# A second feed-forward layer recast in units of 768 tokens, with seven products for both of its matrices

## The chip, the core and the metric

The kernel runs on one core of a Trainium2 chip. The metric is device time in microseconds (us), from start to end of one execution; the median of several runs is compared. TensorE multiplies matrices into PSUM; VectorE, ScalarE and GpSimd (in the rows PE, DVE, ACT and POOL; PEld is TensorE's weight load) do elementwise work; SyncE (SP) issues nearly all DMA. Each engine runs its own instructions in program order and waits on semaphores of the others.

## What is computed

Attention over 4 x 8 heads of 576 tokens and 64 features with a block-causal mask, then two feed-forward layers on 2304 tokens of 512 features, all in float32 (cut from the reference):

```python
attn_out = _attn_ref(**attn_kwargs)             # 4 x 8 x 576 x 64
x = attn_out.transpose(0, 2, 1, 3).reshape(2304, 512)
h = x @ w_in                                    # layer 1: 512 x 2048
g = np.maximum(h, 0.0) + alpha * np.minimum(h, 0.0)
x = g @ w_out                                   # 2048 x 512
h = x @ w2_in                                   # layer 2
g = h * (1.0 / (1.0 + np.exp(-1.702 * h)))
out = g @ w2_out
```

The weights arrive as 64-bit floats. One product in float32 quality is made of three fast ones: each operand is split into a high part and the rest, and high x high, high x rest and rest x high are summed in PSUM. So every operand costs a copy on ScalarE (`hi_part`) and a subtraction on VectorE or GpSimd (`lo_part`) before TensorE can use it.

## The kernel before

The kernel has three stretches that overlap. **Attention** with the first half of layer 1 (8 of its 16 hidden blocks of 128) fills about the first 400 us. **Layer 1's late part** is the other 8 hidden blocks for all tokens, in units of 512 tokens (the order of units is 0, 1, 4, 2, 3, and unit 4 has 256 tokens). **Layer 2** is the same loop again over 5 units and all 16 hidden blocks, with another activation.

A late job is one pair of hidden blocks for one unit. Its first matrix is taken as a 2 x 2 block product with seven block products in place of eight: `comb` makes seven sums of weight blocks early and writes them to DRAM (`wcs`), `load_wc` brings the seven back for each job (7 DMAs of 256 KB), `comb_x` makes the seven sums of the input once per unit, and `prod` (line 838) runs one block product, six matmuls of 256 columns. `first_half`, `snap`, `second_half` and `sums` add the seven into two hidden blocks; `gate` and `gate_split` apply the activation and split it; `g2` (line 904) multiplies with the second matrix in the ordinary way, 12 matmuls of 512 columns for each hidden block. Unit 4 has only four block products per job. In layer 2 the second matrix is loaded, turned to float32 (`narrow`) and split (`split_w`) once, and stays on chip.

What sets the order: every step is put in a list with a place (`at`), and `arrange` (line 1080) plays the list through with a table of costs per instruction and fixes one order per engine; `SHIFT` (line 60) is a table of numbers added to the places, which act as priorities. Pools of tiles (`wts_b`, `xin`, `ps_o`, `ps_n`) open for the late part when attention has ended.

## Time and profile before

| | |
|---|---|
| median of 3 runs | 1004.02 us (1003.83 to 1005.17) |
| span of the profiled execution | 998.3 us |
| outside the span, median less span | 5.7 us |
| PE busy | 979.7 us, 98% |
| DVE busy | 596.3 us, 60% |
| ACT busy | 536.5 us, 54% |
| POOL busy | 359.1 us, 36% |
| DMA | 198.29 MB, mean 199 GB/s |

The span is one profiled execution, from its first to its last instruction. A matmul's busy time holds its way through the array, so matmuls in a stream overlap; what a matmul costs in a stream is read from the distance between starts. A row of the chain with xN is a run of N such matmuls, and its length divided by N is that distance.

### The profile page before, as it was taken

Reading aid. Unit: us, or ns where it says so; the run is one execution under the profiler, and the core shown is the slowest. Engines: PE = TensorE matmul, PEld = TensorE weight load, DVE = VectorE, ACT = ScalarE, POOL = GpSimd, SP = SyncE. Lnnn points to the kernel's source line nnn. Section 1 sums busy time; section 2 is a strip of 40 time slices with the busy share of each in tenths; the row PEclk is TensorE's granted clock in tenths of the full one; section 3 lists DMA queues with packets and bytes.
Section 4 is the critical chain, followed back from the end, with each engine's and each line's share of the span. In section 5 each row is a group of like instructions: output and inputs, shape, how many; then the busy total and the mean of one; then the engine's idle time right before and its main releaser. Section 6 shows DMA issues by size and latency. Waiting matters only on the chain.

```text
span 998.3 us, 21739 instructions
## 1 busy us (share of the span) xinstructions
PE 979.7 (98%) x8260; PEld 860.9 (86%) x8260; DVE 596.3 (60%) x1189; ACT 536.5 (54%) x1284; POOL 359.1 (36%) x396
## 2 busy tenths in 40 slices
PE   8999999999999999999999999999999999999998
PEld 5777877787888999999899989889999899899997
DVE  4788876786677564668777787665424423433321
ACT  4778777775777454555554555554424423433233
POOL 4346234442625156754435445243212411212000
PEclk9999999999999999999999999999999999999999
DMA  9645999999986866754655787986645756564360
GB/s 194 157 127 141 207 222 199 207 205 215 195 199 131 169 209 212 269 188 168 234 190 172 256 299 266 343 279 215 229 159 183 265 164 198 194 207 142 101 205 32
DMA packets 234646, 198.29 MB, mean 199 GB/s; under 512 B 146224, under 2 KB 172848, under 8 KB 234544
## 3 DMA queue, kind: packets, MB, share of 16 engines
q1 hardware_dynamic: 233216, 196.60, 69.2%
q8 instruction: 65, 1.06, 0.5%
q10 hardware_dynamic: 1328, 0.33, 0.2%
q14 instruction: 37, 0.30, 0.1%
HBM read 136.32 MB, written 40.89 MB: 178 GB/s over the span
## 4 chain that ended last, share of the span: by engine, by line
PE 84%; DMA 7%; ACT 3%; DVE 3%; SPq 1%; issue 1%; POOL 0%; ACTq 0%; DVEq 0%; POOLq 0%
PE acc L920 28%; PE ga L845 16%; PE ep L845 11%; PE h L225 8%; PE pv L601 3%; PE sc L450 3%; PE x L270 3%; PE x L271 3%; PE x L272 3%; DMA pt<-hl 3%; PE pv L526 2%; PE tp L390 1%; PE s L450 1%; DMA rw<-in_moe_w_in_dram 1%; PE et L492 1%; DMA xa<-xo 1%
## 5 line engine op out<-in xcount | busy, mean ns | idle before, releaser
L920 PE MATMUL acc<-wh,gs 128*128 128x512 f32 x576 | 184.6, 391 | 0.9 <-DVE o L930 0.9
L845 PE MATMUL ga<-xc,ws 128*128 128x256 f32 x1368 | 184.3, 283 | 0.0
L845 PEld LDWEIGHTS ga<-xc,ws 128*128 128x128 f32 x1368 | 176.3, 192 | 4.6
L845 PE MATMUL ep<-xc,ws 128*128 128x256 f32 x936 | 130.7, 284 | 0.0
L920 PEld LDWEIGHTS acc<-wh,gs 128*128 128x128 f32 x576 | 108.4, 188 | 22.8 <-DVE o L930 1.1
L871 POOL TENSOR_TENSOR v<-u,v 128x256 f32<-128x256 f32 x48 | 44.1, 918 | 229.2 <-ACT v L870 229.2
L845 PEld LDWEIGHTS ep<-xc,ws 128*128 128x128 f32 x936 | 120.6, 192 | 0.3
L920 PE MATMUL acc<-wl,gs 128*128 128x512 f32 x288 | 112.6, 391 | 0.0
L869 ACT ACTIVATE u<-ga 128x512 f32<-128x512 f32 x48 | 28.5, 594 | 148.5 <-PE ga L845 148.4
L143 DVE TENSOR_TENSOR gs<-g,gs 128x512 fp32r<-128x512 f32 (+1 forms) x80 | 65.1, 814 | 68.8 <-ACT gs L140 68.1
L143 POOL TENSOR_TENSOR gs<-g,gs 128x288 fp32r<-128x288 f32 x64 | 56.6, 887 | 101.8 <-ACT gs L140 98.1
L920 PE MATMUL acc<-gs,wh 128*128 128x512 f32 (+1 forms) x320 | 91.9, 370 | 0.5 <-DVE o L930 0.5
L140 ACT ACTIVATE gs<-g 128x288 fp32r<-128x288 f32 (+2 forms) x144 | 75.3, 524 | 19.9 <-DVE g L240 15.3
L225 PE MATMUL h<-xh,wh 128*128 128x288 f32 x256 | 79.1, 309 | 1.5 <-DVE g L240 1.5
L893 DVE TENSOR_TENSOR u<-ep,v 128x256 f32<-128x256 f32 x48 | 20.2, 421 | 99.0 <-PE ep L845 96.2
L270 PE MATMUL x<-gs,wh 128*128 128x288 f32 x256 | 77.5, 305 | 1.1 <-DVE g L240 0.6
L225 PE MATMUL h<-xlb,wh 128*128 128x288 f32 x256 | 77.5, 303 | 0.0
L225 PE MATMUL h<-xh,wl 128*128 128x288 f32 x256 | 76.6, 299 | 0.0
L271 PE MATMUL x<-gs,wh 128*128 128x288 f32 x256 | 76.4, 300 | 0.0
L272 PE MATMUL x<-gs,wl 128*128 128x288 f32 x256 | 76.4, 301 | 0.0
L464 DVE TENSOR_REDUCE stat<-sc 128x1 f32<-128x384 f32 (+7 forms) x128 | 55.1, 457 | 23.8 <-PE sc L450 23.5
L474 ACT ACTIVATE e<-sc,stat 128x384 f32<-128x384 f32 (+7 forms) x128 | 64.1, 511 | 7.4 <-DVE stat L464 6.7
(118 smaller groups left out, 2061.0 us busy)
## 6 DMA issues: line engine op xcount, KB each, us to landing
ws<-wc SPq DMA_DIRECT2D x284, 256.0 KB, 3.9
wc<-wc SPq DMA_DIRECT2D x84, 256.0 KB, 3.3
rw<-in_moe_w_in_dram SPq DMA_DIRECT2D x32, 512.0 KB, 4.2
rw<-in_moe_w_out_dram SPq DMA_DIRECT2D x32, 512.0 KB, 4.4
xa<-xo SPq DMA_DIRECT2D x32, 144.0 KB, 3.4
out_dram<-o SPq DMA_DIRECT2D x18, 256.0 KB, 2.4
nat_k<-in_k_dram SPq DMA_DIRECT2D x32, 128.0 KB, 3.1
vt<-in_v_dram SPq DMA_DIRECT2D x32, 128.0 KB, 3.2
```

What stands on the lines that cost most here:

```text
L140: act.activation(out=dst, in_=src, func=ACTF.Copy, scale=scale_)
L143: eng.tensor_tensor(out=dst, in0=src, in1=hi.bitcast(F32), op=ALU.subtract)
L225: pe.matmul(ps, st_[:, sl], mv[:, c], start=z == 0, stop=z == 3 * KD - 1)
L270: pe.matmul(ps, oh[:, sl], gh, start=f == 0, stop=False)
L271: pe.matmul(ps, oh[:, sl], gl, start=False, stop=False)
L272: pe.matmul(ps, ol[:, sl], gh, start=False, stop=f == NA - 1)
L450: pe.matmul(to[x:x + 64], qs[64 * h:64 * h + 64, 64 * y:64 * y + 64], ks[64 * h:64 * h + 64, k0:k0 + n], start=True, stop=True)
L464: dve.tensor_reduce(out=stat[:, 0, a:a + 1], in_=v, op=ALU.min, axis=AX.X if y < 8 else AX.XY)
L474: act.activation(out=eo if y < 8 else eo.rearrange("p (a b) -> p a b", a=2), in_=v, func=ACTF.Exp, scale=-1.0, bias=stat[:, 0, a:a + 1], a ...
L845: pe.matmul(ps, st_, mv, start=first and z == 0, stop=last and z == 5, skip_group_check=True)
L871: pool.tensor_tensor(out=v, in0=u[:, TH:TB], in1=v, op=ALU.subtract)
L920: pe.matmul(ps, a, b_, start=first and z == 0, stop=last and z == 2)
```

## The change

Layer 2 is written anew. Its tokens go in three units of 768, so a block product of the first matrix (`prod`) has 384 columns. All jobs of a unit run first; their activations stay on chip for the whole unit (`gb`, sixteen tiles of 768 columns). Then the second matrix is done as seven block products too: `g_sum` makes sums of the activations, `g_comb` splits them into one of seven slots, `t_load` and `t_split` bring the second matrix's sums, `g_prod` runs nine matmuls of 256 columns per block product, and `g_post` joins the four output quarters from the accumulators `a`, `b` and `d` and stores them. The second matrix's sums are made by `comb_t` in layer 1's late part and written to DRAM (`w2c` split, `w2s` whole). All weights of layer 2 come back through eight slots of 512 KB (`w_slot`), two block products to a DMA. The late tiles are ranges of bytes in a few large tiles (`late_tile`, `wquad`), some of them those of the early weights. `narrow` takes one form for both layers, which leaves out one VectorE instruction for each of layer 1's 32 weight tiles. The late part of layer 1 keeps its products. `SHIFT` has new numbers throughout, and `arrange` new costs for DMA.

```diff
-    "comb 2": 232.8, "comb 3": 44.7, "first": 27.1, "gate": -98.0, "gate 0": -19.6, "gate 2": 13.1,
...
+    "comb 2": 560.8, "comb 3": 4.3, "comb 4": -41.4, "first": 14.4, "first l0": 104.2, "first l1": 3.4,
...
-    TH = TB // 2
+    HB = TB // 2
+    TT = 768
+    TH = TT // 2
+    LOP = ()
+    WHOLE = (1, 2, 3)
...
+    w1s = [dram.tile([128, 7168], F32, name=f"wc1_{j}") for j in range(NPAIR[1] // 2)]
+    w2c = [dram.tile([128, 7168], F32, name=f"wk{j}") for j in range(NPAIR[1] // 2)]
+    w2s = [dram.tile([128, 3584], F32, name=f"wt{j}") for j in range(NPAIR[1] // 2)]
...
-        if u[0] == 0:
-            act.activation(out=sq, in_=wf[:, :, 1], func=ACTF.Copy, scale=2.0 ** -112)
-        else:
-
-            act.activation(out=sq, in_=wf[:, :, 1], func=ACTF.Prelu, scale=2.0 ** -112, alpha=2.0 ** 32)
...
-        if u[0] == 0:
-            dve.scalar_tensor_tensor(out=a, in0=hi, scalar=-0x80000000, in1=a, op0=ALU.bitwise_and, op1=ALU.bitwise_or)
...
+    def late_tile(tag, dtype=F32R):
+        if (tag, dtype) not in late:
+            n = {"s": 3584, "wo": 8192, "xa": 6144, "sc": 4608, "gs": 4608, "xl0": 2304, "xlb": 1152, "xh0": 1152}.get(tag, 4096)
+            src = late["n"] if tag in ("s", "wo", "xa", "sc") else blk if tag[0] in "gx" else wts_a
+            late[tag, dtype] = src.tile([128, n], dtype, tag=tag, name=f"l_{tag}")
+        return late[tag, dtype]
...
+    def sums_of(l, io, c11, c12, c21, c22, r):
+        if (l, io) == (1, 1):
+            return {4: (r, c12, c11, ALU.subtract), 6: (None, c22, c12, ALU.subtract), 5: (c11, c22, r, ALU.subtract),
+                    3: (None, c21, c11, ALU.subtract)}, {0: c11, 1: c21, 2: c22}
+        return {4: (r, c21, c22, ALU.add), 6: (None, c11, c21, ALU.subtract), 5: (c11, r, c11, ALU.subtract),
+                2: (None, c12, c11, ALU.subtract)}, {0: c11, 1: c12, 3: c22}
...
+    def comb_t(j, z):
+        i = MAKE[z]
+        a, b = (words[1, f, 1] for f in fpair(1, j))
+        if i == 0:
+            words[1, j, "r"] = raw.tile([128, 256], F32, tag="wr", bufs=1, name="wr")
+        two_, one_ = sums_of(1, 1, *quarters(a, b), words[1, j, "r"])
+        whole = i in WHOLE
+        t = wc_tile((1, 2 * j, 1), whole)
+        if i in two_:
+            r, x, y, op = two_[i]
+            if r is None:
+                r = t[:, 1] if whole else t[:, 1].bitcast(F32)
+            (dve if i % 2 else pool).tensor_tensor(out=r, in0=x, in1=y, op=op)
+        else:
+            r = one_[i]
+        if whole:
+            o = 512 * i + 256 * (j % 2)
+            sp.dma_start(out=w2s[j // 2][:, o:o + 256], in_=r)
+        else:
+            hi_part(t[:, 0], r)
+            lo_part(pool if i % 2 else dve, t[:, 1], r, t[:, 0])
+            o = 1024 * i + 512 * (j % 2)
+            sp.dma_start(out=w2c[j // 2][:, o:o + 512], in_=t.bitcast(F32).rearrange("p h c -> p (h c)"))
...
+        z = 512 * (7 * (j % 2) + PORD.index(i))
+        sp.dma_start(out=w1s[j // 2][:, z:z + 512], in_=t.bitcast(F32).rearrange("p h c -> p (h c)"))
...
+    def w_slot():
+        z = w_at[0] % 8
+        w_at[0] += 1
+        t = wquad(z - 1)[:, 3072:4096] if z in (1, 2) else late_tile("xa")[:, 1024 * (z and z - 2):][:, 0:1024]
+        return t.rearrange("p (y h c) -> p y h c", y=2, h=2)
...
+    def load_x(u):
+        for z in range(4):
+            r, h = z // 2, z % 2
+            t = late_tile("w2", F32)[:, 768 * z:768 * z + 768].rearrange("p (c t) -> p c t", c=2)
+            xr[u, z] = t
+            sp.dma_start(out=t, in_=x2s[256 * r:256 * r + 256, u + TH * h:u + TH * h + TH].rearrange("(c p) t -> p c t", p=128))
...
+        two_ = {4: (r, b12, b11), 6: (b12, b22, b12), 5: (b11, b22, r), 3: (b21, b21, b11)}
+        one_ = {0: b11, 1: b21, 2: b22}
+        if i in two_:
+            x, y0, y1 = two_[i]
+            pool.tensor_tensor(out=x, in0=y0, in1=y1, op=ALU.subtract)
+        else:
+            x = one_[i]
+        z, o = {0: (late_tile("xl0"), 0), 4: (late_tile("s"), 0), 5: (late_tile("s"), 1536), 1: (wquad(0), 0), 6: (wquad(0), 1536),
+                2: (wquad(1), 0), 3: (wquad(1), 1536)}[i]
+        t = z[:, o:o + 1536].rearrange("p (h c t) -> p h c t", h=2, c=2)
+        hi_part(t[:, 0], x)
+        lo_part(dve, t[:, 1], x, t[:, 0])
+        xc[u, i] = t
...
+    def prod(ps, w, x, first, last):
+        z = 0
+        for c in range(2):
+            sl = slice(128 * c, 128 * c + 128)
+            for st_, mv in ((w[:, 0, sl], x[:, 0, c]), (w[:, 0, sl], x[:, 1, c]), (w[:, 1, sl], x[:, 0, c])):
+                pe.matmul(ps, st_, mv, start=first and z == 0, stop=last and z == 5, skip_group_check=True)
+                z += 1
...
+    def part_a(p):
+        u, j = jobs[p]
+        late_buffers()
+        a, d = (cbank()[:, 0:TH] for _ in range(2))
+        b = bank("b")[:, 0:TH]
+        job[p] = [a, b, d]
+        for i, ps, first in ((0, a, True), (5, b, True), (4, d, True), (1, a, False)):
+            prod(ps, jw.pop((p, i)), xc[u, i], first, i == 1)
+            if i == 0:
+                t = jt[3 * (p % 2)]
+                act.activation(out=t, in_=a, func=ACTF.Copy)
+                job[p].append(t)
+            if i == 5:
+                t = jt[3 * (p % 2) + 1]
+                dve.tensor_tensor(out=t, in0=b, in1=job[p][3], op=ALU.add)
+                job[p].append(t)
+
+    def part_b(p):
+        u, j = jobs[p]
+        a, b, d, p1, uu = job[p][:5]
+        prod(b, jw.pop((p, 6)), xc[u, 6], False, False)
+        q = jt[3 * (p % 2) + 2]
+        dve.tensor_tensor(out=q, in0=b, in1=p1, op=ALU.add)
+        c22 = gb[2 * j + 1][:, TH:]
+        dve.tensor_tensor(out=c22, in0=d, in1=q, op=ALU.add)
+        job[p].append(c22)
+
+    def part_c(p):
+        u, j = jobs[p]
+        a, b, d, p1, uu = job[p][:5]
+        prod(d, jw.pop((p, 2)), xc[u, 2], False, True)
+        c12 = gb[2 * j][:, TH:]
+        dve.tensor_tensor(out=c12, in0=d, in1=uu, op=ALU.add)
+        prod(b, jw.pop((p, 3)), xc[u, 3], False, True)
+        c21 = gb[2 * j + 1][:, 0:TH]
+        dve.tensor_tensor(out=c21, in0=b, in1=p1, op=ALU.add)
+        job[p] += [c12, c21]
...
+    def g_sum(u, j, i):
+        two_, _ = gsum(u, j, i)
+        o, x, y, op = two_[i]
+        dve.tensor_tensor(out=o, in0=x, in1=y, op=op)
+
+    def g_comb(u, j, i):
+        two_, one_ = gsum(u, j, i)
+        x = two_[i][0] if i in two_ else one_[i]
+        t = gc_slot()
+        hi_part(t[:, 0], x)
+        lo_part(dve, t[:, 1], x, t[:, 0])
+        gcs[u, j, i] = t
...
+    def t_split(u, j, i):
+        r, t = gw.pop((u, j, i)), w_slot()
+        hi_part(t[:, :, 0], r)
+        lo_part(pool if i in LOP else dve, t[:, :, 1], r, t[:, :, 0])
+        for y in range(2):
+            gw[u, j + y, i] = t[:, y]
...
+    def g_prod(u, j, i):
+        key = {0: "a", 1: "a", 5: "b", 6: "b", 3: "b", 4: "d", 2: "d"}[i]
+        first, last = i in (0, 5, 4) and j == 0, i in (1, 3, 2) and j == NPAIR[1] - 1
+        if first:
+            acc[u, key] = [cbank() for _ in range(2)]
+        ps = acc[u, key]
+        g, w = gcs.pop((u, j, i)), gw.pop((u, j, i))
+        for m in range(3):
+            sl = slice(128 * m, 128 * m + 128)
+            o = 256 * (m % 2)
+            to, ops = ps[m // 2][:, o:o + 256], ((g[:, 0, sl], w[:, 0]), (g[:, 0, sl], w[:, 1]), (g[:, 1, sl], w[:, 0]))
+            for z, (st_, mv) in enumerate(ops):
+                pe.matmul(to, st_, mv, start=first and z == 0 and m != 1, stop=last and z == 2, skip_group_check=True)
...
+                dve.tensor_tensor(out=t[:, x:y], in0=ps, in1=(acc[u, "p1"] if i in "uq" else t)[:, x:y], op=ALU.add)
+        if i in ("p1", "u", "q"):
+            return
+        r, h = int(i[0]), int(i[1])
+        sp.dma_start(out=out[u + TH * r:u + TH * r + TH, 256 * h:256 * h + 256].rearrange("(m p) d -> p m d", p=128),
+                     in_=t.rearrange("p (m d) -> p m d", m=3))
...
+    for u in range(0, NT, TT):
+        at("load x", n - (9 if u else 4.5), lambda u=u: load_x(u), L)
+        for z, i in enumerate(XORD):
+            at("split x 2", n - 3 + 0.4 * z, lambda u=u, i=i: comb_x(u, i), L)
+        for j in range(kp):
+            p = len(jobs)
+            jobs.append((u, j))
+            m = n + J * j
+            for z in range(14):
+                if z % 2 == 0 and z // 7 == j % 2:
+                    y = z % 7
+                    at("load wc", m - 1.5 + Q * y + (0.6 if y > 4 else 0), lambda p=p - j % 2, c=z // 2: job_w(p, c), L)
+            at("first", m, lambda p=p: part_a(p), L)
+            at("snap", m + 1.2, lambda p=p: part_b(p), L)
+            c = J + 0.8 if j < kp - 1 else 1.25
+            at("second", m + c, lambda p=p: part_c(p), L)
...
+        seq = [(j, 0) for j in range(kp)]
+        seq += [(j + y, i) for j in range(0, kp, 2) for i in (5, 4) for y in range(2)]
+        seq += [(j, i) for i in (6, 1, 2, 3) for j in range(kp)]
+        for z, (j, i) in enumerate(seq):
+            m = n + Q * z
+            lag = 1.5
...
+    seq_w += [(t_end + NR + 1 + (n2 + 14 - t_end - NR) * j / NPAIR[1], 1, 0, j) for j in range(NPAIR[1])]
+    seq_w += [(n2 + 15 + (n3 + 4 - n2 - 15) * j / NPAIR[1], 1, 1, j) for j in range(NPAIR[1])]
...
-                t = size / run * (8.3 + 0.0368 * run) / 16
+                t = size / run * (12 + 0.0415 * run) / 16
```

In layer 2 before, TensorE's row of work for one job (`ga` and `ep` are the job's two PSUM banks, `xc` and `ws` sums of input and weights, `acc` the output, `wh` and `wl` the second matrix's parts):

```order
L845 MATMUL ga<-xc,ws 128x256 x12
L845 MATMUL ep<-xc,ws 128x256 x6
L845 MATMUL ga<-xc,ws 128x256 x12
L845 MATMUL ep<-xc,ws 128x256 x12
L920 MATMUL acc<-wh_9775,gs 128x512
L920 MATMUL acc<-wl_9776,gs 128x512
L920 MATMUL acc<-wh_9775,gs 128x512 x2
```

In the changed kernel, TensorE where the last job of the second unit (L1094, accumulators `b` and `c`) meets that unit's products of the second matrix (L1210; `l_sc` holds the split activations, `l_xa` and `w` the slots of weights):

```order
L1094 MATMUL b<-w_651,w_745 128x384 x6
L1094 MATMUL c_10599<-w_651,w_745 128x384 x6
L1210 MATMUL c_10681<-l_xa,l_sc 128x256 x6
L1210 MATMUL c_10682<-l_xa,l_sc 128x256 x3
L1210 MATMUL c_10681<-l_xa,l_sc 128x256 x6
L1210 MATMUL c_10682<-l_xa,l_sc 128x256 x2
L1094 MATMUL b<-w_745,l_xa 128x384 x6
L1210 MATMUL c_10682<-l_xa,l_sc 128x256
```

The 512-column matmuls of layer 2 are gone; job after job of 384 columns is followed by a long run of 256-column products.

VectorE in such a run of products of the first unit, in the changed kernel (L160 is a split: of activations into `l_sc` or `l_xl`, of weights from `st`; L1166 is a sum of activations, L1225 joins an output):

```order
L160 TENSOR_TENSOR l_xa<-st,l_xa 128x2x256
L160 TENSOR_TENSOR l_sc<-l_w_8887,l_sc 128x384
L160 TENSOR_TENSOR l_xa<-st,l_xa 128x2x256
L160 TENSOR_TENSOR l_xl_8728<-l_w_8887,l_xl_8728 128x384
L1166 TENSOR_TENSOR l_w_8887<-l_w_8887 128x384
L160 TENSOR_TENSOR l_sc<-l_wo,l_sc 128x384
L1166 TENSOR_TENSOR l_w_8887<-l_w_8887 128x384
L1166 TENSOR_TENSOR l_wo<-l_wo,l_w_8887 128x384
L160 TENSOR_TENSOR l_sc<-l_wo,l_sc 128x384 x4
L1225 TENSOR_TENSOR l_gs<-c_9568,l_gs 128x512
```

And before, VectorE in a job of layer 2 (`wl` is the split of the second matrix, `gs` that of the activations, `wa` and `sq` the turning of weights to float32):

```order
L893 TENSOR_TENSOR u<-ep,v 128x256
L894 TENSOR_TENSOR u<-u,ga 128x256
L895 TENSOR_TENSOR ep<-ep,u 128x256
L896 TENSOR_TENSOR ga<-ga,u 128x256
L143 TENSOR_TENSOR wl_9449<-sq,wh_9448 128x512
L143 TENSOR_TENSOR gs<-g,gs 128x512
L175 TENSOR_SCALAR wa<-sq 128x512
```

The splits of activations, four sums and one split per weight tile have become seven splits and four sums per pair of hidden blocks and the splits of three of the seven weight sums in every unit.

## Rows read from the trace of the kernel before

**Rows 1.** Windows: busy us (instructions) of each engine, granted clock, DMA share, GB/s
```profile
core 0: us, PE busy (x) PEld busy (x) DVE busy (x) ACT busy (x) POOL busy (x), PEclk, DMA share, GB/s
400.00:600.00 200.00, 198.95 (x1330) 183.86 (x1329) 147.68 (x273) 105.88 (x231) 99.36 (x106) 1.00 0.66 223
0.00:350.00 350.00, 337.56 (x4108) 271.42 (x4108) 252.85 (x584) 243.54 (x682) 140.37 (x174) 0.99 0.84 183
...
600.00:650.00 50.00, 49.12 (x313) 44.59 (x312) 34.28 (x62) 29.88 (x54) 20.55 (x20) 1.00 0.85 303
650.00:994.00 344.00, 344.00 (x2149) 311.92 (x2147) 131.98 (x229) 129.32 (x256) 68.70 (x69) 1.00 0.56 184
```
**Rows 2.** The chain of work that ended last: start, length, what
```profile
392.31 6.41 PE h L225 x48
...
845.42 1.44 PE ep L845 x12
846.86 5.47 PE acc L920 x24
```
**Rows 3.** Groups by line: form and count, busy us, mean ns, idle before
```profile
L920 PE MATMUL acc<-wh,gs 128*128 128x512 f32 x576 | 184.6, 391 | 0.9 <-DVE o L930 0.9
L845 PE MATMUL ga<-xc,ws 128*128 128x256 f32 x1368 | 184.3, 283 | 0.0
...
L845 PE MATMUL ep<-xc,ws 128*128 128x256 f32 x936 | 130.7, 284 | 0.0
...
L920 PE MATMUL acc<-wl,gs 128*128 128x512 f32 x288 | 112.6, 391 | 0.0
```
**Rows 4.** Timeline, PE where layer 2 begins: start, length, what [idle before]
```profile
599.01 1.60 PE L845 MATMUL ga<-xc,ws 128*128 128x256 f32 x12
...
633.50 0.50 PE L920 MATMUL acc<-wh,gs 128*128 128x512 f32 x1 [0.88 <-DVE o L930]
```
**Rows 5.** Timeline, the end: ACT's copies and SP's stores
```profile
993.70 1.28 ACT L933 ACTIVATE o<-acc 128x512 f32<-128x512 f32 x2 [3.23 <-PE acc L920]
...
994.32 1.02 SPq L934 DMA_DIRECT2D out_dram<-o  x2
```
**Rows 6.** Timeline of DVE around 578 us
```profile
575.72 0.69 DVE L143 TENSOR_TENSOR xc<-xt,xc 128x512 fp32r<-128x512 f32 x1
576.32 0.68 DVE L143 TENSOR_TENSOR gs<-ga,gs 128x512 fp32r<-128x512 f32 x1
...
580.44 0.41 DVE L894 TENSOR_TENSOR u<-u,ga 128x256 f32<-128x256 f32 x1
580.77 0.42 DVE L895 TENSOR_TENSOR ep<-ep,u 128x256 f32<-128x256 f32 x1
```
**Rows 7.** Groups of DVE by line, 400 to 600 us
```profile
L179 DVE SCALAR_TENSOR_TENSOR sq<-rw,wa 128x512 int32<-128x512 int32 x17 | 13.5, 793 | 0.3
...
L143 DVE TENSOR_TENSOR wc<-wc 128x256 fp32r<-128x256 f32 x21 | 10.1, 482 | 9.5 <-ACT wc L140 9.3
...
L175 DVE TENSOR_SCALAR wa<-sq 128x512 int32<-128x512 int32 x17 | 8.6, 508 | 1.9 <-ACT sq L173 1.0 <-DMA wc<-wc 0.8
L747 DVE TENSOR_TENSOR wc<-sq 128x256 f32<-128x256 f32 x14 | 8.4, 599 | 3.6 <-DMA wc<-wc 3.5
```
**Rows 8.** Windows of 10 us, as rows 1
```profile
570.00:580.00 10.00, 10.00 (x64) 9.04 (x63) 9.89 (x17) 5.53 (x11) 6.81 (x6) 1.00 0.77 245
580.00:590.00 10.00, 10.00 (x74) 9.47 (x74) 8.94 (x19) 5.79 (x12) 2.95 (x4) 1.00 1.03 359
```
**Rows 9.** Timeline, DVE and POOL in one job of layer 2
```profile
880.17 0.74 POOL L872 TENSOR_TENSOR u<-u,v 128x256 f32<-128x256 f32 x1
...
880.22 1.23 DVE L143 TENSOR_TENSOR gs<-g,gs 128x512 fp32r<-128x512 f32 x1 [0.73 <-ACT gs L140]
...
889.29 0.69 DVE L143 TENSOR_TENSOR gs<-g,gs 128x512 fp32r<-128x512 f32 x1 [1.66 <-ACT gs L140]
```
**Rows 10.** What PE waited for, 0 to 350 us: total, times, longest
```profile
PE pv L601 <- DMA pt<-hl: 5.5, 7, 2.0
```

More of the change, by code (lines that the diff above doesn't have):

```diff
@@ L922, in block_out @@
[L922 to L934 removed]
+            for z, (a, b_) in enumerate(((oh[:, sl], gh), (oh[:, sl], gl), (ol[:, sl], gh))):
+                pe.matmul(accs[key][d][:, 0:n], a, b_, start=first and z == 0, stop=last and z == 2)
@@ new lines, in job_gate, with gsum @@
+    def job_gate(p, y):
+        u, j = jobs[p]
+        g = gb[2 * j + (y == 2)]
+        to = (g[:, 0:TH], g[:, TH:], g)[y]
+        act.activation(out=to, in_=job[p][0] if y == 0 else to, func=ACTF.Gelu_apprx_sigmoid)
+    gcs = {}
+    gw = {}
+    def gsum(u, j, i):
+        t0_, t1_ = gb[2 * j], gb[2 * j + 1]
+        h = slice(0, TH), slice(TH, 2 * TH)
+        c11, c12, c21, c22 = t0_[:, h[0]], t1_[:, h[0]], t0_[:, h[1]], t1_[:, h[1]]
+        r = g1[j % 2]
+        sub, add = ALU.subtract, ALU.add
+        two_ = {4: (r, c21, c22, add), 6: (c21, c11, c21, sub), 5: (c11, r, c11, sub), 2: (c12, c12, c11, sub)}
+        return two_, {0: c11, 1: c12, 3: c22}
@@ L959 @@
-        if j == NPAIR[l] - 1:
+            at("gemm2", place[p + 2] + 0.1 + 0.1 * y, lambda u=u, f=f, a=j == 0 and y == 0, b=j == NPAIR[0] - 1 and y == 1: g2(u, f, a, b))
+        if j == NPAIR[0] - 1:
             at("out", place[p + 2] + 0.4, lambda u=u: block_out(u))
     for u in units:
-        n = start[u[3]]
-        at("load x", n - 8, lambda u=u: load_x(u))
-        for y, i in enumerate(XC if u[2] == TB else (0, 1)):
-            at("split x 2", n - 2 + 0.1 * y, lambda u=u, i=i: comb_x(u, i))
@@ L968 @@
[L968 to L972 removed]
+        n = start[u[2]]
+        at("load x", n - 8, lambda u=u: load_x1(u))
+        for y, i in enumerate(XC if u[1] == TB else (0, 1)):
+            at("split x 2", n - 2 + 0.1 * y, lambda u=u, i=i: comb_x1(u, i), after=n - 0.08 + 0.01 * y if i in (1, 3, 4, 6) else None)
```

474 lines of the change are left out of this document (293 added, 181 removed), and 6 rows, old and new, of the table SHIFT.

## The prediction

> **What bounds the kernel now.** I read the windows first. In 650 to 994 us, which is layer 2 alone, PE is busy in all 344.00 us, while DVE is busy in 131.98, ACT in 129.32 and POOL in 68.70 of them, and the DMA share is 0.56 [rows 1]. So there the time is the number of matmuls times their distance, and nothing else. From 400 to 600 us PE is busy in 198.95 of 200, but DVE already in 147.68 (74%) [rows 1]. In the first 350 us PE is idle for 12.4 us (350 less 337.56), and the largest single wait behind that, 5.5 us in seven pieces, is for a DMA of the attention [rows 1, 10]. The granted clock is 0.99 to 1.00 in all of these, the upper of the two levels, so the clock has nothing to give [rows 1]. The kernel is bound by PE, and a change pays by taking distance out of PE's row. It pays for as long as the other engines can prepare operands at the new pace.
>
> The busy time of a group does not give that distance: one 512-column matmul counts as 391 ns busy [rows 3], yet 24 of them in the chain take 5.47 us, so 227.9 ns each [rows 2]. Twelve of 256 columns take 1.44 us, so 120 ns, and 48 of 288 columns take 6.41 us, so 133.5 ns [rows 2]. I work with these. There is no row for 384 columns. Its distance lies between the last one and 227.9; on the straight line between 288 and 512 columns (0.421 ns a column) it is 133.5 + 96 x 0.421 = 174.0 ns.
>
> **PE's work in layer 2.** Before: the 576 + 288 matmuls of 512 columns whose moving operand is the second layer's `gs` [rows 3] take 864 x 0.2279 = 196.9 us. Of L845 there are 1368 + 936 = 2304 in all [rows 3]; layer 1 has 16 full jobs of 42 and 4 small ones of 24, 768, which leaves 1536 x 0.120 = 184.3 us. Together 381.2 us. As a test of this arithmetic: layer 2's first matmul starts at 599.01 [rows 4] and the last output copies begin at 993.70, the last store at 994.32 [rows 5], so some 395.3 us. In them lie also the last two `g2` of layer 1, 48 x 0.228 = 10.9 us, and 3.2 us remain for idle time, of which 0.88 is one wait for a DVE copy [rows 4]. So the sum accounts for the stretch to 1%.
>
> After: 24 jobs of seven block products of six matmuls are 1008 x 0.174 = 175.4 us, and three units of 56 block products of nine are 1512 x 0.120 = 181.4 us, 356.8 us together. **PE gains 24.4 us.** Most comes from the second matrix: seven products in place of eight, and no unit of 256 tokens with its four products for three quarters of the gain of seven. If 384 columns cost 165 or 183 ns (5% either way), this is 9 us more or less.
>
> **What the other engines must do for it.** One unit of 768 tokens now takes PE 58.5 us of jobs (8 x 7.31) and 60.5 us of products, 119.0 us. DVE starts instructions of 512 columns 0.60 us apart (575.72 to 576.32) and of 256 columns 0.33 us apart (580.44 to 580.77) [rows 6], which puts 384 columns at 0.465 and 768 at 0.87 us. For one unit: 8 jobs x 5 additions x 0.465 = 18.6; 32 sums of activations x 0.465 = 14.9; 56 splits of them x 0.465 = 26.0; 12 splits of weight sums x 0.60 = 7.2; 5 joins of the output, 0.93 each, 4.7; 7 splits of the input x 0.87 = 6.1. That is 77.5 of 119.0 us, 65%, and so it fits on the whole. The halves differ: in a unit's products alone (nearly all sums, the splits, the weights, the joins, part of the input) I count some 55.9 of 60.5 us, 92%. So there is a slack of 4.6 us in each such half, and the order must be good. ACT has one copy for each split and less of the rest, about 40 of 67 us where they are densest; it follows DVE.
>
> How firm are DVE's durations? The same 512-column split took 1.23 us at 880.22, beside an addition on POOL at 880.17, and 0.69 us at 889.29 with none there [rows 9]. The Trainium skill (GPSIMD Engine Reference, section 1, Specifications) says that GpSimd shares its SBUF interfaces with VectorE and that the two contend when a VectorE instruction has two SBUF inputs, as these splits have; that pair of rows agrees with it. In the changed kernel POOL has almost nothing in the products but the next unit's input sums, so I keep the short durations and make the long one a rival.
>
> Between jobs and products PE meets operands that depend on the last job's activation, and at a unit's end the accumulators must be joined before their banks are used again. The program's row of work interleaves there: the last job's `b` waits while products of earlier hidden blocks run. Three units have two such places each. A wait like the 0.88 us of [rows 4] at half of them is 3 us; nothing at all is the one bound, 2 us at each of six places, 12 us, the other. **I take +3.**
>
> **Layer 1's late part.** The second matrix's preparation moves here. From 400 to 600 us 17 narrowings ran [rows 7]; eleven more come in from later, each 0.508 + 0.793 us, 14.3 us. The sums and splits of `comb_t` add for seven pairs about 2 x 0.599 + 3 x 0.48 us each, 18.5 us; eight of L747's go, 4.8 us [rows 7]. So DVE goes from 147.68 [rows 1] to about 176 of 200 us, 88%. That is close, but the work has a whole layer's length to be done in, and in 570 to 580 us PE was busy in 10.00 us beside a DVE busy in 9.89 [rows 8], so a dense DVE does not by itself hold PE up. Bounds: 0 where it all fits, and 12 us where the part above 88% turns into delay of the gates in half of the jobs. **I take +3.** The new DMA writes go on SP's queue; the share there was 0.66 [rows 1].
>
> **The weights' way back.** A job of layer 2 reads 1.835 MB. Before, a full job took 42 x 0.120 + 24 x 0.228 = 10.5 us with its `g2`; now jobs follow each other every 7.31 us, so 251 GB/s in the job halves and less in the products. The trace moved 303 GB/s over 600 to 650 us at a share of 0.85 [rows 1] and 359 over 580 to 590 [rows 8]. So I take 0 here, with the eight slots of 512 KB in front as the cover; without it, see the second rival.
>
> **The start and the end.** L178's 32 instructions go, 24.7 us of DVE in all (0.77 each), but no wait of PE in the first 350 us that I found ends with them; the longest sum of waits is for `pt` [rows 10]. DVE was busy there in 252.85 of 350 us [rows 1]. I put that at 0. The new numbers in `SHIFT` reorder the attention as well, though PE's work there is the same: the 12.4 us of idle time may shrink (at best by about 8, since the first loads are needed in any order) or grow as much. **I take -1.** At the end two copies by ACT (1.28 us for both) and a store of 256 KB stand last [rows 5]; after it are a join by DVE of 512 and 256 columns, 0.93 us, and a store of 384 KB. **+0.8**, between 0 and 2.
>
> **Sum.** 998.3 - 24.4 + 3 + 3 - 1 + 0.8 = 979.7 us of span. Around the span lie 5.7 us (median 1004.02 less 998.3). So **985.4 us**, 1.9% faster. The terms' own bounds are wide in the late part and the joins (0 to 12) and in the start (-8 to +8); all would hardly fall to one side, and I give this case 975 to 992.
>
> **The rivals.**
>
> First, VectorE sets the pace of the products. If the 56 splits start 0.62 us apart and not 0.465, a third longer, where POOL's neighbourhood alone made one 1.8 times as long [rows 9], a half needs 55.9 + 8.7 = 64.6 us against PE's 60.5. That is 4.1 us three times, 12.3; it takes the place of the 3 us for joins: 994.7, still faster. It decides from 4.6 us more per half. For it speak the 92%; against it, that POOL is idle for most of these halves and that the sums can begin while jobs still run.
>
> Second, the slower side: the weights' feed sets the pace of the jobs. The gain of 18.6 us (1004.0 - 985.4) is eaten when each of 24 jobs takes 0.78 us longer, 8.08 us, which is 227 GB/s. At 220, hardly under what 400 to 600 us moved with 0.66 of the engines [rows 1], a job takes 8.34 us, 24.8 us are lost, and the time is 1010. For it: reads and stores and the next unit's input share the queues, and a slot can be refilled only when the product that reads it has ended, so eight slots are four products' worth of time in practice. Against it: the 303 and 359 GB/s [rows 1, 8].
>
> Third, the attention's new order gives back most of PE's idle time there: -8 in place of -1, so 978.
>
> Fourth, the change doesn't bring what it counts: the late part and the joins both near their bound of 12, 985.4 + 18 = 1003.4, no change.
>
> Fifth, the distance of matmuls may not go by columns as I took it. With fewer columns per matmul something is lost if long matmuls are the cheaper ones per column. In these rows 512 columns cost 0.445 ns each, 288 cost 0.464 and 256 cost 0.469 [rows 2], so the loss is small and is in the sum. Were a 512-column matmul much cheaper, the gain on PE would vanish and only the +5.8 us of the other terms would stay: 1009.8. The Trainium skill (TensorE: Matmul & The Clock Gate, section Back-to-back issue gap) gives, for sustained streams, about 81 ns for 128 columns and 131 ns for 512; on a line between these, 256 and 384 columns would be 98 and 114 ns, and layer 2 would go from 263.2 to 262.9 us, an estimate from that page: no gain. The rows show 120 and 227.9 ns and speak against it.
>
> **How the numbers follow.** Forecast, 975 to 992: 0.66. VectorE's pace, about 995: 0.14. Feed, about 1010: 0.08. Attention, about 978 and below: 0.07. No change, about 1003: 0.03. The distance rule, 1009.8: 0.02. About 0.2% is what a measurement of this kernel can tell from no change, 2 us here. Faster is forecast, VectorE's pace and attention, less a hundredth for a VectorE worse than priced: 0.86. Same, 0.04. Slower, feed and rule: 0.10. The range runs from 974 to 998: below, a little under the attention's case; above, just over VectorE's; it leaves out the last three cases and some of each tail.
>
> **What would show it.** In the changed profile the chain should hold runs of 384 columns at 174 ns a matmul; layer 2 from its first matmul to its last should take about 360 us with PE busy in all but a few of them; and 400 to 600 us should have a DVE near 88% and PE still above 97%. Idle time before L1210 put down to DVE's or ACT's splits would mean the first rival; idle time before L1094 put down to DMA the second; fewer than 6 us of idle time in the first 350 us the third. I am wrong if the 384 columns are off the line, or if the late part of layer 1 turns DVE's load into waits of PE beyond 12 us.

## The result, and the profile after

The changed kernel takes 980.1 us (median of four runs, 978.9 to 983.8), 0.977 of the kernel before (95% interval 0.974 to 0.980). Forecast were 985.4 us, within 974 to 998. A second set of runs gave 981.6 us and 0.979 (0.976 to 0.981). The profiled execution spans 977.0 us, 21.3 less than before.

The windows of the changed kernel, in the stretches of [rows 1] (columns as there):

```profile
core 0: us, PE busy (x) PEld busy (x) DVE busy (x) ACT busy (x) POOL busy (x), PEclk, DMA share, GB/s
0.00:350.00 350.00, 339.71 (x4128) 272.69 (x4129) 237.88 (x562) 245.66 (x688) 144.18 (x175) 1.00 0.81 185
...
400.00:600.00 200.00, 197.97 (x1322) 182.68 (x1323) 172.83 (x318) 119.99 (x261) 109.46 (x120) 1.00 0.82 280
600.00:650.00 50.00, 49.44 (x261) 45.60 (x260) 35.62 (x58) 21.50 (x38) 14.48 (x9) 1.00 0.93 340
650.00:970.00 320.00, 319.97 (x2299) 319.65 (x2298) 227.71 (x429) 161.11 (x305) 11.91 (x6) 1.00 0.69 226
```

PE is as full as before; what shrank is its row of work. VectorE (DVE) is the engine that grew: 228 of 320 us in layer 2, where it was 132 of 344, and 173 of 200 us in the late part of layer 1, where it was 148.

Layer 2 by halves of its three units (jobs, then products, from the first unit's jobs on):

```profile
608.00:677.70 69.70, 69.70 (x396) 67.27 (x396) 44.47 (x75) 29.04 (x52) 10.46 (x8) 1.00 0.87 303
677.70:734.30 56.60, 56.60 (x473) 56.60 (x473) 50.99 (x100) 32.79 (x65) 4.13 (x2) 1.00 0.64 216
734.30:796.80 62.50, 62.50 (x371) 62.50 (x370) 34.08 (x59) 26.52 (x47) 3.89 (x2) 1.00 0.82 277
796.80:853.40 56.60, 56.60 (x473) 56.60 (x472) 49.94 (x100) 32.70 (x65) 0.00 (x0) 1.00 0.65 207
853.40:913.50 60.10, 60.07 (x347) 59.75 (x347) 29.33 (x55) 20.95 (x38) 0.00 (x0) 1.00 0.79 257
913.50:972.60 59.10, 59.10 (x495) 59.10 (x494) 47.83 (x97) 33.35 (x66) 0.00 (x0) 1.00 0.45 141
```

In the products DVE is busy for some 50 of 56.6 us, nine tenths, while PE never stops. From the chain of waits, the rows that answer [rows 2] (start, length, what):

```profile
677.68 56.63 PE c L1210 x472
734.31 1.04 PE c L1094 x6
735.36 1.04 PE b L1094 x6
...
738.48 1.04 PE c L1094 x6
...
740.05 1.07 PE c L1094 x6
...
853.39 1.04 PE c L1094 x6
```

472 matmuls of 256 columns in 56.63 us are 120.0 ns each. Six of 384 columns take 1.04 us, 174 ns by the distance of their starts. From the second unit's first job (734.31) to the third's (853.39) are 119.08 us; 58.5 + 60.5 = 119.0 were counted. The only waits of PE behind the late part of layer 1, and the end (timeline of DVE and SP):

```profile
PE b L1094 <- ACT l_s L157: 0.6, 1, 0.6
```
```profile
972.57 1.02 DVE L1225 TENSOR_TENSOR l_gs<-c,l_gs 128x512 f32<-128x512 f32 x2 [6.21 <-PE c L1210]
973.62 0.37 SPq L1229 DMA_DIRECT2D out_dram<-l_gs  x1
```

**Where the 21.3 us came from.** I cut each trace in three, at the first matmul of layer 2 and at the last matmul. What PE still has to do for layer 1 at the first cut (matmuls left times their distance) is counted to the part ahead.

| us | before | after | difference | forecast |
|---|---|---|---|---|
| first matmul of layer 2 | 601.2 | 599.0 | | |
| work of layer 1 left there | 10.9 | 14.6 | | |
| ahead of layer 2 (sum of the two) | 612.1 | 613.6 | +1.5 | -1 + 3 |
| layer 2 (rest, to the start of the last matmul) | 381.9 | 359.0 | -22.9 | -24.4 + 3 |
| from there to the end of the span | 4.3 | 4.4 | +0.1 | +0.8 |
| span | 998.3 | 977.0 | -21.3 | -18.6 |

The line of layer 2 is firm and the line ahead of it is not. By the same cut layer 2 of the kernel before takes 381.5 and 382.4 us in two other runs below (the one in the old order and the one with a planner cost moved; 386.8 in a third, with a new plan), and layer 2 of the changed kernel takes 357.3 to 359.0 us in all seven runs that leave it as it is. The part ahead ends at 616.2 us when the changed kernel runs again, so there +1.5 could as well be +4.1.

### The profile page after: what moved, and what is told of

The parts are those of the page before. It is cut to its first block, busy times and chain, and to the rows that moved or that the text cites. A ratio compares the mean times of both kernels' runs of the same rounds, so it can differ in the third digit from the quotient of the medians.

```text
span 977.0 us, 22224 instructions
## 1 busy us (share of the span) xinstructions
PE 957.8 (98%) x8380; PEld 870.1 (89%) x8380; DVE 699.0 (72%) x1405; ACT 574.7 (59%) x1353; POOL 311.3 (32%) x341
## 5 line engine op out<-in xcount | busy, mean ns | idle before, releaser
L1210 PE MATMUL c<-l_xa,l_sc 128*128 128x256 f32 x1026 | 129.0, 283 | 0.0
L1210 PEld LDWEIGHTS c<-l_xa,l_sc 128*128 128x128 f32 x1026 | 126.2, 192 | 0.0
L256 PE MATMUL h<-xh,w 128*128 128x288 f32 x512 | 113.5, 305 | 2.8 <-DVE g L285 2.7
L1010 PE MATMUL c<-gs,l_wo 128*128 128x512 f32 (+1 forms) x480 | 108.8, 371 | 0.6 <-ACT gs L157 0.4
L256 PEld LDWEIGHTS h<-xh,w 128*128 128x128 f32 x512 | 83.7, 188 | 12.2 <-issue 6.9
L1010 PEld LDWEIGHTS c<-gs,l_wo 128*128 128x128 f32 x480 | 82.1, 189 | 13.6 <-ACT gs L157 0.8
L160 POOL TENSOR_TENSOR gs<-g,gs 128x288 fp32r<-128x288 f32 x64 | 57.5, 903 | 93.7 <-ACT gs L157 62.2
L312 PE MATMUL x<-gs,w 128*128 128x288 f32 x256 | 76.5, 301 | 1.1 <-DVE g L285 1.1
L313 PE MATMUL x<-gs,w 128*128 128x288 f32 x256 | 76.7, 301 | 0.0
L256 PE MATMUL h<-xlb,w 128*128 128x288 f32 x256 | 76.7, 299 | 0.0
L314 PE MATMUL x<-gs,w 128*128 128x288 f32 x256 | 76.3, 299 | 0.0
L506 DVE TENSOR_REDUCE stat<-sc 128x1 f32<-128x384 f32 (+7 forms) x128 | 54.4, 457 | 24.8 <-PE sc L492 24.4
L516 ACT ACTIVATE e<-sc,stat 128x64 f32<-128x64 f32 (+7 forms) x128 | 64.1, 512 | 4.0 <-DVE stat L506 3.8
L617 DVE SCALAR_TENSOR_TENSOR hl<-e,stat,hl 128x320 f16<-128x320 f32 (+8 forms) x108 | 56.6, 576 | 6.8 <-ACT hl L612 6.6
L285 DVE SCALAR_TENSOR_TENSOR g<-g,nalph,h 128x288 f32<-128x288 f32 x64 | 32.6, 509 | 37.2 <-ACT g L283 35.6
L160 DVE TENSOR_TENSOR l_sc<-l_wo,l_sc 128x384 fp32r<-128x384 f32 x84 | 48.2, 578 | 11.2 <-ACT l_sc L157 11.0
L312 PEld LDWEIGHTS x<-gs,w 128*128 128x128 f32 x256 | 48.0, 188 | 4.0 <-DVE g L285 2.0
L313 PEld LDWEIGHTS x<-gs,w 128*128 128x128 f32 x256 | 48.3, 189 | 2.4 <-issue 2.2
```

The costliest lines, as they stand in the source:

```text
L160: eng.tensor_tensor(out=dst, in0=src, in1=hi.bitcast(F32), op=ALU.subtract)
L256: pe.matmul(ps, st_[:, sl], mv[:, c], start=z == 0, stop=z == 3 * KD - 1)
L312: pe.matmul(ps, oh[:, sl], gh, start=f == 0, stop=False)
L313: pe.matmul(ps, oh[:, sl], gl, start=False, stop=False)
L314: pe.matmul(ps, ol[:, sl], gh, start=False, stop=f == NA - 1)
L506: dve.tensor_reduce(out=stat[:, 0, a:a + 1], in_=v, op=ALU.min, axis=AX.X if y < 8 else AX.XY)
```

## The experiments

Theory A: the gain is PE's shorter row in layer 2 and nothing else. Its rivals: part of it comes from the leaner `narrow`, or from the new order ahead of layer 2; and VectorE, the feed or the price of a matmul are nearer to the edge than counted. Theory B comes out of the first runs.

**The changed kernel again**, as the base of the runs beside it. Expected: 

> The changed kernel once more, as the base of the three that run beside it. Its trace gave a span of 977.0 us; 980.1 us was the median. Theory A (TensorE's row is the bound, all of the gain comes from layer 2's matmuls): ratio to before 0.975 to 0.979. The rival that the first result was a chance of its four runs: the ratio moves by more than 0.003.

Measured: 981.6 us, 0.979 (0.976 to 0.981), span 979.5. The result stands; a repetition can't tell A from its rivals. One caution: layer 2's first matmul starts at 601.6 us here, at 599.0 in the first profile, and at 600.7 and 606.3 in two runs below whose order is the same up to there. One execution's start of layer 2 says nothing to within 7 us.

**Both forms of `narrow` put back.**

```diff
-        act.activation(out=sq, in_=wf[:, :, 1], func=ACTF.Prelu, scale=2.0 ** -112, alpha=2.0 ** 32)
+        if u[0] == 0:
+            act.activation(out=sq, in_=wf[:, :, 1], func=ACTF.Copy, scale=2.0 ** -112)
+        else:
+            act.activation(out=sq, in_=wf[:, :, 1], func=ACTF.Prelu, scale=2.0 ** -112, alpha=2.0 ** 32)
...
+        if u[0] == 0:
+            dve.scalar_tensor_tensor(out=a, in0=hi, scalar=-0x80000000, in1=a, op0=ALU.bitwise_and, op1=ALU.bitwise_or)
```

Expected: 

> The changed kernel with the two forms of `narrow` put back: 32 more VectorE instructions in layer 1, some 0.77 us each by the trace of before, 24.7 us in all, half of them before 120 us. Theory A: TensorE never waits for them, so within 2 us of the changed kernel either way. Rival: the leaving out is what paid for the denser VectorE of 400 to 600 us (172.8 of 200 us busy); then this one is 3 us or more slower than the changed kernel.

Measured: 1003.9 us, ratio to before 1.000 (0.999 to 1.002). The whole gain is gone, 22 us, by 25 us of an engine that PE was not seen to wait for. Its windows:

```profile
400.00:500.00 100.00, 92.93 (x623) 86.01 (x622) 72.47 (x126) 56.13 (x126) 58.87 (x64) 0.98 0.79 252
500.00:600.00 100.00, 93.75 (x612) 86.53 (x611) 89.61 (x172) 57.59 (x129) 51.94 (x55) 0.97 0.86 292
```

PE is idle for 13.3 us between 400 and 600, against 2.0, though DVE is busy in fewer of them (162.1, against 172.8), and all 32 instructions lie ahead of 400 us. So it is not simply their time. But the edit has a second effect: `arrange` (the function that fixes each engine's order) plans with the longer list, and the same numbers in `SHIFT` give another order on every engine.

**The old numbers for the attention.** Here only the order changes, and no work.

```diff
-    "gemm1": 72.2, "gemm1 0": 301.6, "half": 71.9, "half 0": -175.6, "norm": 250.5,
+    "gemm1": 68.3, "gemm1 0": 171.6, "half": 66.8, "half 0": 164.8, "norm": 32.7,
...
```

Expected: 

> The changed kernel with the numbers in `SHIFT` that order the attention and the first half of layer 1 as they were before; the late part keeps the new ones. In the first 400 us TensorE was busy in 387.3 us before and 387.5 in the changed kernel. Theory A: the new numbers bring nothing there, within 2 us of the changed kernel. Rival: the order of the attention gives part of the gain; 3 to 8 us slower than the changed kernel.

Measured: 1009.5 us, 1.006 (1.004 to 1.008), 28 us behind the changed kernel. The windows show that the attention itself is not the loser: PE is busy for 339.37 us in the first 350, as in the changed kernel; the loss lies behind it, in the late part, where it is idle for 19.4 us of 200, and the granted clock is down to 0.96 there.

```profile
0.00:350.00 350.00, 339.37 (x4108) 270.21 (x4109) 237.21 (x558) 243.70 (x682) 142.79 (x175) 1.00 0.82 183
400.00:600.00 200.00, 180.65 (x1160) 164.48 (x1161) 160.50 (x291) 112.38 (x249) 108.83 (x118) 0.96 0.80 268
```

Layer 2 is the same in both of these runs by the cut of the table above, 358.0 and 357.3 us. **Theory B**: the numbers in `SHIFT` fit one list of instructions, and what was lost is the fit.

**One cost of the planner moved by half a per cent**, in both kernels. The work is the same to the instruction.

```diff
-DRAIN = 190
+DRAIN = 191
```

Expected of the changed kernel: 

> The changed kernel with one cost in `arrange` moved by half a per cent, DRAIN from 190 to 191 ns, and no instruction more or less: the same numbers in `SHIFT` now give another order in all engines. Theory B (the gain needs the very order that the numbers were fitted to, and any other loses 10 us or more in the late part of layer 1): 988 to 1005 us. Rival (this kernel bears small changes of order, and the two runs that lost 22 and 28 us lost them by what they changed): within 4 us of the changed kernel.

Expected of the kernel before: 

> The kernel before with the same cost moved, DRAIN 190 to 191 ns. Its late part has VectorE busy for 147.7 of 200 us, against 172.8 in the changed kernel. Theory B, with the denser late part as the reason for the frailty: the kernel before loses less by another order, 0 to 8 us. Rival (any fitted order is worth 20 us, in both kernels alike): 15 us or more slower than before, and the change is worth its 24 us on any order.

Measured: the changed kernel 991.3 us, 0.987 (0.984 to 0.991); the kernel before 1016.4 us, 1.012 (1.009 to 1.015). Another order costs 10 and 13 us. That before loses as much speaks against the denser late part as the reason. The difference between the two with nudged orders is 25.1 us, between the two fitted ones 23.9 and 21.4 in the two sets of runs; one pair, while the changed kernel's own orders so far lie anywhere from 980 to 1010 us, so I take no more from it than that the gain does not hang on the fit alone. Where it is lost in the changed kernel, in three windows of 10 us, the wait with the most time from 500 to 600 us (engine, line, releaser: total, times, longest), two rows of the timeline in that wait, and the chain behind it:

```profile
530.00:540.00 10.00, 8.53 (x72) 8.33 (x71) 6.77 (x11) 5.11 (x12) 6.92 (x7) 1.00 0.97 341
540.00:550.00 10.00, 3.77 (x28) 3.33 (x26) 9.97 (x20) 3.90 (x10) 6.39 (x7) 0.75 0.74 249
550.00:560.00 10.00, 10.00 (x55) 8.98 (x53) 8.21 (x18) 5.93 (x14) 3.36 (x5) 0.74 1.01 348
```
```profile
PE c L1010 <- ACT gs L157: 6.5, 2, 6.2
```
```profile
547.47 0.74 DVE L285 SCALAR_TENSOR_TENSOR ga<-l_sc,nalph,ga 128x512 f32<-128x512 f32 x1
548.07 0.67 ACT L206 ACTIVATE l_w<-rw 128x512 f32<-128x512 f32 x1
```
```profile
549.27 2.27 PE c L1010 x4
551.54 2.63 PE ga L944 x12
```

DVE is full for 10 us and PE stands, because an activation's split comes late. Two queues hold that split. The activation itself (L285) had its input from ScalarE at 536.2 us, and DVE came to it only at 547.47; the split's copy then stood on ScalarE behind a narrowing's (L206), which had waited for its load. Behind the gap the granted clock is 0.74 for 10 us in which PE is busy throughout: twelve matmuls of 256 columns take 219 ns each, against 120 at the full clock. With the four of 512 columns ahead of them they take 4.90 us, where the distances at the full clock make 2.35; that is some 2.5 us on top of the gap of 6.2. The loss is one gap and its wake, not a steady drag.

**The 32 instructions without another order.** They are kept from the planner and put in behind their forerunners afterwards.

```diff
+            EXTRA[before_.name] = nc.cur_bb.bb.instructions[-1]
...
+        if i.name in extra:
+            continue
...
+                if todo[k][0].name in EXTRA:
+                    orders[e].append(EXTRA[todo[k][0].name])
```

Expected: 

> The two forms of `narrow` again, the same 32 more VectorE instructions, but left out of the plan and put in behind their forerunner afterwards, so that every engine has exactly the changed kernel's order around them. With them in the plan the kernel was 22 us slower than the changed one. Theory B (the order, not the work, was what was lost): within 4 us of the changed kernel, 980 to 985 us. Rival (the 32 instructions themselves, 24.7 us of VectorE, are what the denser late part can't bear): 995 to 1005 us again.

Measured: 995.5 us, 0.991 (0.988 to 0.994): 14 us slower than the changed kernel, where B had at most 4. So in this order the instructions do cost, more than half of their time. The last matmul of the attention starts at 357.7 us, at 348.1 without them, and layer 2's first at 616.9, at 601.6 without them; layer 2 is as long as ever, 358.8 us. That DVE's work for PE is queued behind these 32 is my reading and only in part shown: PE's waits for DVE's activations `g` came to 6.3 us in the first 400, against 3.9. B as I had put it falls; what stands is that the new order has no room for them. Whether the changed kernel would bear them with numbers fitted to them, no run shows.

**The reverse, in the kernel before.** First with a new plan, then with its own order kept (an instruction of one column stands in each place, and the plan counts it as the long one):

```diff
-            dve.scalar_tensor_tensor(out=a, in0=hi, scalar=-0x80000000, in1=a, op0=ALU.bitwise_and, op1=ALU.bitwise_or)
+            dve.scalar_tensor_tensor(out=a[:, 0:1], in0=hi[:, 0:1], scalar=-0x80000000, in1=a[:, 0:1], op0=ALU.bitwise_and,
+                                     op1=ALU.bitwise_or)
+            FULL.add(nc.cur_bb.bb.instructions[-1].name)
```

Expected with a new plan: 

> The kernel before with the one form of `narrow`: 32 VectorE instructions less, 24.7 us, and a new order by the old numbers. By the prediction's step (no wait of TensorE ends with them) the work is worth 0; what is seen is the order's share: 0 to 8 us slower. Rival: the leaving out is worth several us by itself, and the kernel is faster than before by 2 us or more.

Expected in the old order: 

> The kernel before with the one form of `narrow`, and exactly the order of before on every engine: in each of the 32 places a VectorE instruction of one column stands for the one of 512 columns, and the plan counts it as the long one. This takes some 22 us off VectorE and moves nothing. By the prediction's step (no wait of TensorE ends with these instructions): within 2 us of before. Rival, from the run in which the same 32 instructions, put into the changed kernel's order, cost 14 us: 5 us or more faster than before.

Measured: with a new plan 1019.7 us, 1.015 (1.012 to 1.018), no better than the nudged order's 1016.4; in the old order 1002.9 us, 0.999 (0.997 to 1.000). DVE is busy 235.56 us in the first 350, against 252.85 in [rows 1], and PE gains nothing:

```profile
0.00:350.00 350.00, 335.52 (x4051) 270.65 (x4052) 235.56 (x582) 242.34 (x679) 138.85 (x173) 0.99 0.84 183
```

So the prediction's step holds for the kernel before: there the leaving out is worth nothing by itself. Put into the changed kernel, where the order does not reckon with them, the same instructions cost 14 us. So an engine's busy share did not tell here whether it had time to spare; the order did.

**The second matrix's sums and splits left out** of the late part of layer 1 (the quarters are stored as they are).

```diff
-            hi_part(t[:, 0], r)
-            lo_part(pool if i % 2 else dve, t[:, 1], r, t[:, 0])
...
-            sp.dma_start(out=w2c[j // 2][:, o:o + 512], in_=t.bitcast(F32).rearrange("p h c -> p (h c)"))
+            sp.dma_start(out=w2c[j // 2][:, o:o + 512], in_=b)
```

Expected: 

> Leaves out the sums and splits of the second matrix in layer 1's late part; its quarters are written to DRAM as they are, by as many bytes, so that layer 2 does the same work on other numbers. It takes some 20 to 35 us of VectorE, ScalarE and GpSimd out of the stretch before layer 2. Theory A with a price for this part (TensorE lost about 2 us more than before between 400 and 600 us): 1 to 3 us faster than the changed kernel. Rival, that the loss there has another cause (the order, the loads and narrowings, the writes): within 1 us of it.

Measured: 984.4 us, 0.980 (0.977 to 0.983), span 980.4: not faster. DVE has 13 us less to do there, and PE is no fuller:

```profile
400.00:600.00 200.00, 196.55 (x1321) 181.27 (x1319) 158.02 (x282) 111.05 (x235) 92.41 (x101) 1.00 0.83 279
```

This alone does not clear the load, since the edit also brought another order, which may hide a gain of some us. The changed kernel's own windows bound it more directly: PE is idle for 2.0 us from 400 to 600 there and for 1.0 before ([rows 1]). So the new work in the late part costs about 1 us of idle time, in the order that was fitted to it. The few us lost ahead of layer 2 have another cause, or none but the scatter of one execution.

**VectorE's edge in the products.**

```diff
-        lo_part(dve, t[:, 1], x, t[:, 0])
+        for _ in range(2 if i in (5, 4, 6) else 1):
+            lo_part(dve, t[:, 1], x, t[:, 0])
```

Expected: 

> The changed kernel with 24 of the 56 splits of activations in each unit done twice (VectorE writes the same numbers again), 24 x 0.47 = 11.3 us more of VectorE per unit, planned for. In a unit's products VectorE is busy 50 of 56.6 us. If all of it stays in the products: 50 + 11.3 - 56.6 = 4.7 us in each of three, 14 us slower than the changed kernel (994 us); by the prediction's own count of 55.9 of 60.5 us it would be 6.7 us each, 20 us (1000 us). If the sums and splits spread into the jobs, where VectorE is busy 34 of 62.5 us: within 4 us of the changed kernel.

Measured: 1021.9 us, 1.017 (1.014 to 1.020), 40 us behind the changed kernel for 34 us of DVE. By unit, from its first job to the next one's, the three are longer by 14, 12 and 11 us. A window over the first unit's products, five of 4 us within it, and pieces of the chain of work from there:

```profile
678.00:751.00 73.00, 65.55 (x483) 63.02 (x482) 70.92 (x130) 38.68 (x74) 8.07 (x4) 0.93 0.55 173
```
```profile
700.00:704.00 4.00, 3.24 (x24) 2.69 (x22) 4.00 (x9) 2.19 (x5) 0.00 (x0) 1.00 0.44 174
704.00:708.00 4.00, 1.68 (x11) 1.22 (x10) 4.00 (x10) 1.96 (x5) 0.00 (x0) 1.00 0.00 0
708.00:712.00 4.00, 3.79 (x17) 3.40 (x18) 4.00 (x9) 1.28 (x3) 0.00 (x0) 0.57 0.00 0
...
716.00:720.00 4.00, 2.76 (x13) 2.76 (x14) 4.00 (x9) 0.94 (x2) 0.00 (x0) 0.50 0.33 78
720.00:724.00 4.00, 4.00 (x28) 4.00 (x28) 3.95 (x8) 1.80 (x4) 0.00 (x0) 0.76 0.92 294
```
```profile
704.48 1.96 DVE l_sc L160 x4
...
708.23 1.97 DVE l_sc L160 x4
...
710.24 1.74 PE c L1211 x7
...
712.61 2.43 DVE l_sc L160 x5
...
717.24 15.15 PE c L1211 x107
```

PE is idle for 73.0 - 65.55 = 7.45 us of this half, and 6.7 is what the prediction's count gives for the dose (55.9 + 11.3 - 60.5). That likeness misleads, since the unit became 14 us longer. What the rows show is VectorE as the pace: it is busy for 70.92 of 73.00 us (67.22 of 69.00 in the second unit), and from 679 to 717 us the chain of work runs mostly through its instructions. DVE has 130 instructions in this half against 100 in the changed kernel, six more than the dose of 24, and 20 us more of busy time against the dose's 11.3. The granted clock adds to it: the gap at 704 us is followed by windows at 0.57 and 0.50, the lower of the two levels being 1.2 GHz. But most of the time at the lower clock PE would have waited for VectorE anyway. Where PE is on the chain, 7 and 107 matmuls take 16.89 us in place of 13.7 at 120 ns each, so the clock cost some 3 us of the 14.

**Half as much again on the queue.**

```diff
+        o = dram.tile([128, 512], F32, name=f"spare{p}_{c}")
+        sp.dma_start(out=o, in_=w1s[j // 2][:, 1024 * c:1024 * c + 512])
```

Expected: 

> The changed kernel with a copy of 256 KB from DRAM to DRAM behind each of layer 2's 84 loads of 512 KB for the jobs, half as much again on the same queue, read by no one. The jobs' halves moved 257 to 303 GB/s with TensorE never waiting. If the feed has room up to the 340 to 360 GB/s seen elsewhere: at 1.5 x 251 = 377 GB/s in the jobs a few us slower, 0 to 8 us, spread over the slots. If the feed was at its edge, as the second rival held: each job is longer by up to half, 24 x 3.6 = 88 us slower.

Measured: 1016.9 us, 1.014 (1.011 to 1.017). This missed its aim. These copies go from DRAM to DRAM and wait for no slot on the chip, so the plan let them run ahead: all 84 were issued between 392 and 570 us, in the late part of layer 1:

```profile
400.00:600.00 200.00, 177.53 (x1186) 164.43 (x1185) 145.61 (x265) 104.15 (x230) 93.17 (x105) 0.96 0.96 331
```

PE is idle for 22 us there, at a share of 0.96, and layer 2's rates from 700 us on are those of the changed kernel (layer 2 is 9 us longer, with PE idle for 5 us in its first 80). It tells nothing of the jobs' feed. It suggests that the late part has no room for 50 GB/s more; the order is another one too, so this is not shown.

**Two matmuls of 192 columns for one of 384.**

```diff
-                pe.matmul(ps, st_, mv, start=first and z == 0, stop=last and z == 5, skip_group_check=True)
+                for y in range(2):
+                    q = slice(192 * y, 192 * y + 192)
+                    pe.matmul(ps[:, q], st_, mv[:, q], start=first and z == 0 and y == 0, stop=last and z == 5, skip_group_check=True)
```

Expected: 

> The changed kernel with each matmul of 384 columns done as two of 192, 1008 more matmuls of the same work. By the prediction's straight line (120 ns at 256 columns, 133.5 at 288, 227.9 at 512): 93 ns each, 186 for 174, 1008 x 12 ns = 12 us slower than the changed kernel. If the time goes by columns alone: no change. If the weight load before each matmul sets a floor near the 109 ns at which 128-column transposes follow each other: 218 for 174, 44 us slower.

Measured: 1038.5 us, 1.035 (1.032 to 1.038), 57 us behind the changed kernel. From its chain:

```profile
762.15 1.34 PE b L1096 x12
763.49 1.00 PE c L1096 x9
```

1.34 us for twelve are 111.7 ns, where the line through 256, 288 and 512 columns gives 93. 1008 x (2 x 111.7 - 174) = 50 us of the 57; of the rest, 5 us are idle time of PE up to 736 us, in the first unit, which the new order brought. A floor near 110 ns, as in the third expectation, is what fits. Whether the floor is the weight load ahead of each matmul or another cost of each instruction, no run here separates.

## Why the prediction was right

**PE's row** was right to the nanosecond: 174 ns on the straight line, 173 to 178 in the rows above; 120.0 ns in the products; 119.08 us a unit for 119.0. Layer 2 became 22.9 us shorter for -24.4 on PE, so what was put at 3 for joins and waits came to 1.5, of which 0.6 is idle time of PE. The whole sum was 2.7 us too high in the span (979.7 for 977.0). The rest of the miss, 985.4 for 980.1, is no part of the kernel. The 5.7 us "around the span" were the median of some executions less the span of another, quicker one: measured execution by execution, time less span is 1.8 to 1.9 us for the changed kernel and 1.9 to 2.5 for the kernel before.

**The late part and the start**, +3 and -1, came out at +1.5 together, and at +4.1 when the kernel ran again. This is the step where the forecast was right by more luck than working. It put the cost on VectorE's load, 88% forecast and 86% measured; the load cost about 1 us of idle time in the order that was fitted to it, while the order, which I had allowed 8 us either way for the attention only, moves the time ahead of layer 2 by far more. By the cut of the table it ends at 613.6 and 616.2 us in the fitted order, 626.2 with the nudged one, 631.5 with both forms put into the fitted order, 640.9 with both forms planned and 646.8 with the old numbers. Layer 2 itself, over all six, keeps within 357.3 and 359.0. So the gain in layer 2 is sure, and whether the kernel shows it depends on an order that nothing in the profile of before could tell. The third rival went the wrong way: it held that the new order might gain 8 us; the other orders that were run lost 10 to 28 us.

**L178 at nothing** was right for the kernel before, by the run in its own order. For the changed kernel the prediction did not reckon with an order that is fitted to the removal and loses 14 us without it.

**The first rival** was closer than its price. The count of VectorE in the products, 92%, was near (50 of 56.6 us, 88 to 90%, in two units, 81% in the third), and so was the slack, 4.6 us for 5.6 and 6.7. What I had missed is what comes with a dose: by the count, 11.3 us more should make a unit 6.7 us longer, and it became 11 to 14 us longer, because the products then held more of VectorE's work than the dose (what of that is the new order's doing, no run shows), and the granted clock took some 3 us in the first unit. The long durations of [rows 9] came up once in the products, 1.61 us for a split of 384 columns, with GpSimd busy for 4.13 us in the first unit's and 0.00 in the others'.

**The second rival** is refuted by the changed profile itself: the jobs' halves moved 257 to 303 GB/s, over the 227 from which the feed would have eaten the gain, and PE waited there once, 0.6 us, for a split. How much room is left stays open, since the run meant for it loaded another stretch.

**The distance of matmuls** went by columns from 256 to 512, as in the sum. The Trainium skill (TensorE: Matmul & The Clock Gate, section Back-to-back issue gap) says that the weight load and the matmul together set the spacing; the run with 192 columns is in keeping with that, but does not separate the two. Its figures do not fit these rows: 131 ns for 512 columns, where they show 227.9.

**A check that I misread.** The prediction took the matmuls at 599.01 [rows 4] for layer 2's first and was left with 3.2 us of idle time. The 18 matmuls that start there are the second half of layer 1's last job, 18 x 0.120 = 2.2 us; layer 2 starts at 601.2, and about 1 us is idle. Nothing of the sum hangs on it.

## What to carry to other kernels

When one engine is full, count its instructions by the distance of their starts, at each size, and interpolate; that gave the size of this gain to 1.5 us. Where a planner fixes the order by fitted numbers, any edit moves two things, the work and the fit: move one planner cost by a hair in both kernels to learn what a fit is worth (here 10 to 13 us), and test an edit of work with the order held. A gap in TensorE's row can cost more than its length, when the granted clock falls behind it and TensorE is what the rest waits for.
